# Attention followed by an MLP on one core: q and k in longer rows, group sums on VectorE, and an earlier reciprocal chain

## The chip, the cores and the metric

The kernel runs on one core of a Trainium2 chip. The metric is the device time of one execution in microseconds (us), lower is better. Timed runs of the kernel before and of another kernel alternate on the same chip. A ratio is the mean time of one kernel's fast runs over that of the other's fast runs of the same rounds, so it is not quite the ratio of the medians that stand beside it. Engine names: TensorE (PE in the profile; PEld is its weight load), VectorE (DVE), ScalarE (ACT), GpSimd (POOL), SyncE (SP).

## The reference

```python
# q, k, v: (8, 8, 576, 64) f32.  w_in: (512, 2048), w_out: (2048, 512)
q_d = q.reshape(B, H, 144, 4, D).mean(axis=3)        # the same for k_d, v_d
out_up = np.repeat(sm_attn(q_d, k_d, v_d), 4, axis=2)  # attention of group means
scores = np.where(abs(pos_i - pos_j) < 4, scale * q @ k.T, -1e9)
out_local = softmax(scores) @ v                        # a narrow band around the diagonal
x = (out_up + out_local).transpose(0, 2, 1, 3).reshape(4608, 512)
h = x @ w_in
out = (h * sigmoid(h)) @ w_out
```

## The kernel before

Heads are treated two at a time, as 32 pairs; four pairs make one batch of 576 tokens. The MLP goes over nine blocks of 512 tokens. Block 0 needs the pairs 0 to 3, block 1 the pairs 4 to 7 as well. For each pair, q and k are loaded, converted to bf16 and transposed by TensorE. First scores (the band) and second scores (of the group means), exponentials on ScalarE, a mask multiply on VectorE, row sums Z, a chain of small DMAs that turns row sums into a broadcast reciprocal, PV (probabilities by v), and the normalised xo and xT follow. In the profiles, duo is the PSUM tile of a pair's transposes, scores and PV; hps and ops are the PSUM tiles of the MLP's two matmuls; th is what ScalarE makes of hps, and gT the product that VectorE makes of both.

An engine carries out its instructions in the order in which they were written: in the traces of the kernel before, VectorE's 373 instructions come in the order of the program, by line and output tile, and so do ScalarE's 359 and, by line, SyncE's 331 DMA issues. This order is made when the kernel is built, by a small list scheduler in the kernel's own source, from a guessed duration (`cost`) of each instruction. So a wait in one engine's queue also delays whatever stands behind it.

The loads of q and k in 512-byte rows, where row c, p, r holds token 192 c + 2 p + r (two tokens of 64 values side by side):

```python
def load_qk(p):
    for nm, t, src in (("qs", qs, q), ("ks", ks, k)):
        P.op("SP", lambda s, t=t, src=src: s.dma_start(
            t[i][:, :, :], src[b, h:h + 2].rearrange("h (c p r) d -> p (h c) (r d)", p=96, r=2)), ...)
```

The transposes, the group sums by a matmul with a constant G, and the copies out of PSUM:

```python
def ph_T(p):
    for x, (nm, st, xt, xd) in enumerate((("q", qb, qT, qd), ("k", kb, kT, kd))):
        tps = D[:, x, 0:288].bitcast(BF16)
        dps = D[:, x, 288:432]
        ...   # six transposes into tps; six matmuls with G_bf into dps
        src = tps[:, :].rearrange("p (c r g) -> p c r g", c=3, r=2)
        dst = xt[j][:, :].rearrange("p (c g r) -> p c r g", c=3, r=2)   # writes every 2nd bf16: a 4-byte step
        if nm == "q":
            # VectorE: tensor_copy(dst, src), then tensor_copy(qd, dps)
        else:
            # ScalarE: activation(dst, src, Copy), then activation(kd, dps, Copy)
```

The reciprocal chain of two pairs (z): row sums to SBUF (zc), four small DMAs (zr), a reciprocal (rr), a DMA to memory (scr) and four broadcasting DMAs (Rb). All of them are issued by SyncE, which also issues all loads of q, k and v and all stores of the output:

```python
P.op("SP", ... zr[i][10*o:10*o+10, :] <- zc ...)        # four
P.op("DVE", lambda e: e.reciprocal(rr[i][:, :], zr[i][:, :]), ...)
P.op("SP", ... scr[i] <- rr[i] ...)
P.op("SP", ... Rb[n][64*h:64*h+64, :] <- scr[i][...].to_broadcast([64, 720]) ...)   # four
```

The softmax here doesn't subtract the row's maximum and nothing guards it: scores larger than these inputs give would overflow.

Of the kernel before, what the change touches and what calls it, by code (L numbers as in the profile page):

```python
# [38 lines left out]
class Prog:  # L39
# [9 lines left out]
    def __init__(self):  # L49
        self.streams = {e: [] for e in self.ENGS}  # L50
        self.know = {e: {} for e in self.ENGS}
        self.dcount = {}
        self.free = {e: 0 for e in self.ENGS}
        self.ring = {"SP": 0, "POOL": 0}
# [28 lines left out]
    def op(self, eng, fn, r=(), w=(), dma=None, cost=0):  # L83
# [24 lines left out]
        if dma:  # L108
            other = self.ring["POOL" if eng == "SP" else "SP"]
            self.free[eng] = max(t + 600, self.ring[eng] - 4000)  # L110
            begin = max(self.free[eng], self.ring[eng])
            self.ring[eng] = begin + cost + min(cost, max(0, other - begin)) // 2
# [65 lines left out]
def bass_hourglass_attn__then__act_silu_kernel(  # L178
# [9 lines left out]
    with kctx:  # L188
# [21 lines left out]
        NST, NVB, NP_, NR, NEARLY = 2, 5, 5, 4, 4  # L210
        qs = sb("qs", [96, 6, 128], F32, NST)
        ks = sb("ks", [96, 6, 128], F32, NST)
        vs = sb("vs", [128, 10, 64], F32, NST)
        vq = sb("vq", [72, 4, 256], F32, NST)
# [6 lines left out]
        kT = sb("kT", [128, S_], BF16, 2)  # L221
        qd = sb("qd", [128, SD], BF16, 2)
# [11 lines left out]
        G_bf = sb("G_bf", [96, 48], BF16)  # L234
# [26 lines left out]
        def const_g():  # L261
            pool(lambda g: g.memset(cf[0:96, 0:48], 0.25), w=[c0])
            pool(lambda g: g.affine_select(out=cf[0:96, 0:48], in_=cf[0:96, 0:48], compare_op=ALU.is_ge,
                                           fill=0.0, base=0, pattern=[[-2, 48]], channel_multiplier=1),
                 r=[c0], w=[c0])
            pool(lambda g: g.affine_select(out=cf[0:96, 0:48], in_=cf[0:96, 0:48], compare_op=ALU.is_ge,
                                           fill=0.0, base=1, pattern=[[2, 48]], channel_multiplier=-1),
                 r=[c0], w=[c0])
            pool(lambda g: g.tensor_copy(G_bf[:, :], cf[0:96, 0:48]), r=[c0], w=[R("G")])
# [17 lines left out]
        def load_qk(p):  # L287
            b, h = divmod(2 * p, H_)
            i = p % NST
            for nm, t, src in (("qs", qs, q), ("ks", ks, k)):  # L290
                P.op("SP", lambda s, t=t, src=src: s.dma_start(  # L291
                    t[i][:, :, :], src[b, h:h + 2].rearrange("h (c p r) d -> p (h c) (r d)", p=96, r=2)),
                    w=[R(f"{nm}{i}")], dma=f"{nm}{i}", cost=1100)

        def load_v(p):
            b, h = divmod(2 * p, H_)
            i = p % NST
            for hh in range(2):
# [4 lines left out]
                     w=[R(f"vs{i}")], dma=f"vs{i}", cost=900)  # L303
            P.op("SP", lambda s: s.dma_start(
                vq[i][:, :, :], v[b, h:h + 2].rearrange("h (s p r) d -> p (h s) (r d)", s=2, r=4)),
                w=[R(f"vq{i}")], dma=f"vq{i}", cost=900)

        def cast(p):
            i, j = p % NST, p % 2
            for nm, a, bb in (("q", qs, qb), ("k", ks, kb)):  # L310
                dst = bb[j][:, :, :, :]
                src = a[i][:, :, :].rearrange("p (h c) x -> p h (c x)", h=2).rearrange(
                    "p h (c d) -> p c h d", d=64)
# [10 lines left out]
        def castv(p):  # L324
            i, m = p % NST, p % NVB
# [24 lines left out]
        def ph_T(p):  # L350
            D, bk = next_duo()
            j = p % 2
            for x, (nm, st, xt, xd) in enumerate((("q", qb, qT, qd), ("k", kb, kT, kd))):
                tps = D[:, x, 0:288].bitcast(BF16)
                dps = D[:, x, 288:432]
                for c in range(3):
                    for r in range(2):
                        w = st[j][:, 2 * c + r, :, :].rearrange("p h d -> p (h d)")
                        P.op("PE", lambda t, c=c, r=r, w=w, tps=tps: t.transpose(  # L359
                            tps[:, 192 * c + 96 * r:192 * c + 96 * r + 96], w, id_bf[:, :]),  # L360
                            r=[R("id"), R(f"{nm}b{j}")], w=[bk[x]], cost=42)
                for c in range(3):
                    for r in range(2):
                        w = st[j][:, 2 * c + r, :, :].rearrange("p h d -> p (h d)")
                        mm(dps[:, 48 * c:48 * c + 48], w, G_bf[:, :], [R("G"), R(f"{nm}b{j}")],
# [414 lines left out]
```

## Time and profile before

The kernel before takes 421.43 us (median of 3 runs, 420.27 to 421.85); its profiled execution has a span of 423.5 us.

| engine | busy, us | share of the span |
|---|---|---|
| TensorE | 355.2 | 84% |
| VectorE | 243.5 | 58% |
| ScalarE | 205.2 | 48% |
| GpSimd | 155.2 | 37% |

From the page of the kernel before; the columns are line, engine, operation, output and input with their shapes, count, then busy us and the mean ns of one, then idle time of the engine before it and what ended it:

```profile
L375 ACT ACTIVATE kT<-duo 128x576 bf16<-128x576 bf16 x32 | 26.3, 821 | 39.8 <-PE duo L347 39.7
L370 DVE COPY qT<-duo 128x576 bf16<-128x576 bf16 x32 | 25.5, 796 | 12.0 <-PE duo L347 11.8
```

These are the two copies out of PSUM: 0.82 us on ScalarE and 0.80 us on VectorE, once per pair.

### The profile page before, as it was taken

What the parts mean: (1) busy time and instruction counts of PE and PEld (TensorE: products, weight loads), DVE (VectorE), ACT (ScalarE), POOL (GpSimd) and SP (SyncE); (2) the same over time, 40 slices, a digit from 0 to 9 for tenths busy, and PEclk for the clock granted to TensorE, in tenths of its full rate; (3) what the DMA queues carried; (4) which work ended last, traced back from release to release, by engine and by line L of the source; (5) the groups of instructions that cost most, each with busy time, mean ns of one, the idle gap of its engine ahead of it and who ended that gap; (6) DMA issues with size and microseconds to landing.
All of it is one profiled execution on the core that took longest, in us unless ns stands there. A gap on an engine that the chain in (4) does not pass through costs nothing.

```text
span 423.5 us, 7628 instructions
## 1 busy us (share of the span) xinstructions
PE 355.2 (84%) x3033; PEld 225.3 (53%) x3072; DVE 243.5 (58%) x373; ACT 205.2 (48%) x360; POOL 155.2 (37%) x185
## 2 busy tenths in 40 slices
PE   2441333798898979999899999999999999999996
PEld 2331222565655646666566656656556565555552
DVE  1434608777667875858776787659448334333320
ACT  4540310485645755555674756736732434434331
POOL 7634546626567452716543567117000000000000
PEclk9999999999699995999999999999999999999999
DMA  9999999698989994798985898642041100101011
GB/s 186 220 338 266 226 204 193 151 225 193 222 207 225 239 213 121 170 244 216 200 193 177 189 249 200 176 131 79 29 161 56 50 26 25 50 26 50 25 51 74
DMA packets 105665, 66.43 MB, mean 157 GB/s; under 512 B 47006, under 2 KB 95134, under 8 KB 105630
## 3 DMA queue, kind: packets, MB, share of 16 engines
q1 hardware_dynamic: 101406, 59.66, 60.4%
q0 software_dynamic: 4224, 6.29, 6.3%
q8 instruction: 24, 0.39, 0.4%
q14 instruction: 11, 0.09, 0.1%
HBM read 58.25 MB, written 9.61 MB: 160 GB/s over the span
## 4 chain that ended last, share of the span: by engine, by line
PE 64%; DMA 14%; DVE 9%; SPq 4%; issue 4%; POOL 2%; ACT 2%; POOLq 0%; ACTq 0%
PE hps L347 27%; PE ops L347 26%; PE duo L347 8%; DMA vq<-in_v_dram 7%; DMA Rb<-scr 5%; PE duo L359 3%; DVE xT L517 3%; DVE Pt L412 2%; DVE xo L498 2%; SPq L291 2%; DMA scr<-rr 1%; DVE xo L500 1%; SPq L302 1%; POOL vt L328 1%; DVE gT L542 1%
## 5 line engine op out<-in xcount | busy, mean ns | idle before, releaser
L347 PE MATMUL hps<-xT,w_in_sb 128*128 128x512 f32 x576 | 182.3, 442 | 1.7 <-DVE gT L542 1.5
L542 DVE SCALAR_TENSOR_TENSOR gT<-th,hps 128x512 bf16<-128x512 f32 x144 | 98.0, 685 | 114.6 <-ACT th L540 114.4
L347 PE MATMUL ops<-w_out_bf,gT 128*128 128x512 bf16 x537 | 139.0, 382 | 4.4 <-issue 3.3
L540 ACT ACTIVATE th<-hps 128x512 f32<-128x512 f32 x144 | 86.2, 598 | 115.3 <-PE hps L347 115.1
L347 PEld LDWEIGHTS hps<-xT,w_in_sb 128*128 128x128 f32 x576 | 108.5, 193 | 35.1 <-DVE gT L542 4.1
L347 PEld LDWEIGHTS ops<-w_out_bf,gT 128*128 128x128 bf16 x576 | 46.5, 98 | 65.6 <-issue 22.6
L326 POOL CAST vb<-vs 128x640 bf16<-128x640 f32 x32 | 24.5, 767 | 66.6 <-PE duo L347 58.6
L375 ACT ACTIVATE kT<-duo 128x576 bf16<-128x576 bf16 x32 | 26.3, 821 | 39.8 <-PE duo L347 39.7
L328 POOL TENSOR_TENSOR vt<-vq 72x512 f32<-72x512 f32 x32 | 43.2, 1349 | 6.2 <-DMA vq<-in_v_dram 6.2
L321 POOL CAST qb<-qs 96x768 bf16<-96x768 f32 x28 | 23.7, 847 | 52.6 <-PE duo L347 34.4
L517 DVE TENSOR_TENSOR xT<-xo 128x576 fp32r<-128x576 f32 (+2 forms) x40 | 39.2, 996 | 1.1
L359 PE MATMUL duo<-id_bf,qb 96*128 96x96 bf16 x192 | 16.7, 235 | 26.4 <-POOL qb L321 18.3
L412 DVE TENSOR_TENSOR Pt<-Pt,mask_bf 128x1152 bf16<-128x1152 bf16 x32 | 32.1, 1006 | 6.9 <-ACT Pt L404 6.9
L389 ACT ACTIVATE Pt<-duo 128x912 bf16<-128x912 f32 x32 | 29.8, 930 | 9.2 <-PE duo L347 9.2
L347 PE MATMUL duo<-qT,kT 64*128 64x112 bf16 (+1 forms) x320 | 21.6, 234 | 14.6 <-DVE xo L498 8.6
L330 POOL TENSOR_TENSOR vd<-vt 72x256 bf16<-72x256 f32 x32 | 31.2, 974 | 4.3
L561 ACT ACTIVATE osb<-ops 128x512 f32<-128x512 f32 x36 | 21.6, 600 | 23.0 <-PE ops L347 22.7
L370 DVE COPY qT<-duo 128x576 bf16<-128x576 bf16 x32 | 25.5, 796 | 12.0 <-PE duo L347 11.8
L359 PEld LDWEIGHTS duo<-id_bf,qb 96*128 96x128 bf16 x192 | 11.7, 113 | 34.4 <-POOL qb L321 18.9
L498 DVE TENSOR_TENSOR xo<-duo,Rb 128x456 f32<-128x456 f32 x32 | 19.9, 623 | 15.6 <-DMA Rb<-scr 10.9
L347 PEld LDWEIGHTS duo<-qT,kT 64*128 64x128 bf16 x320 | 12.2, 102 | 27.2 <-DVE xo L498 11.7
L321 POOL CAST kb<-ks 96x768 bf16<-96x768 f32 x28 | 23.6, 842 | 7.0 <-DMA ks<-in_k_dram 7.0
(55 smaller groups left out, 261.7 us busy)
## 6 DMA issues: line engine op xcount, KB each, us to landing
Rb<-scr SPq DMA_DIRECT2D x60, 180.0 KB, 4.0
vs<-in_v_dram SPq DMA_DIRECT2D x64, 160.0 KB, 5.4
qs<-in_q_dram SPq DMA_DIRECT2D x32, 288.0 KB, 5.4
ks<-in_k_dram SPq DMA_DIRECT2D x32, 288.0 KB, 6.3
vq<-in_v_dram SPq DMA_DIRECT2D x32, 288.0 KB
out_dram<-osb SPq DMA_DIRECT2D x36, 256.0 KB, 2.2
w_in_sb<-in_moe_w_in_dram POOLq DMA_DIRECT2D x4, 1024.0 KB, 13.4
w_out_bf<-in_moe_w_out_dram POOLq DMA_DIRECT2D x4, 512.0 KB, 8.8
```

Source lines behind the costliest of these rows:

```text
L321: pool(lambda g, d=dst, s=src: g.tensor_copy(d, s), r=[R(f"{nm}s{i}")], w=[R(f"{nm}b{j}")], cost=830)
L328: pool(lambda g: g.tensor_tensor(vt[:, :, :], vq[i][:, :, 0:128], vq[i][:, :, 128:256], ALU.add), r=[R(f"vq{i}")], w=[R("vt")], cost=1290)
L330: pool(lambda g: g.tensor_tensor(vd[m][:, :, :], vt[:, :, 0:64], vt[:, :, 64:128], ALU.add), r=[R("vt")], w=[R(f"vd{m}")], cost=750)
L347: return P.op("PE", lambda t: t.matmul(out_, lhsT, rhs, start=start, stop=stop, skip_group_check=True), r, w, cost=cost)
L359: P.op("PE", lambda t, c=c, r=r, w=w, tps=tps: t.transpose(tps[:, 192 * c + 96 * r:192 * c + 96 * r + 96], w, id_bf[:, :]), r=[R("id"), R( ...
L375: P.op("ACT", lambda e, src=src, dst=dst: e.activation(dst, src, AF.Copy), r=[bk[x]], w=[R(f"kT{j}")], cost=650)
L389: P.op("ACT", lambda e: e.activation(Pt[m][:, :, 0:456], D[:, :, 0:456], AF.Exp, scale=0.125), r=bk, w=[R(f"P{m}")], cost=930)
L412: P.op("DVE", lambda e: e.tensor_tensor(Pt[m][:, :, :], Pt[m][:, :, :], mask_bf[:, :].unsqueeze(1).to_broadcast([128, 2, S_]), ALU.mult), ...
L498: P.op("DVE", lambda e: e.tensor_tensor(xo[x][:, 0:456], D[:, 0, 0:456], Rb[u][:, 0:456], ALU.mult), r=[bk[0], R(f"Rb{u}")], w=[R(f"xo{x}" ...
L517: P.op("DVE", lambda e, dst=dst, in0=in0, in1=in1: e.tensor_tensor(dst, in0, in1, ALU.add), r=[R(f"xo{x}")], w=xblk(kc, t, e_), cost=180 + n)
L540: P.op("ACT", lambda e: e.activation(th[tb][:, :], hps[hb][:, :], AF.Tanh, scale=0.5), r=[R(f"h{hb}", True)], w=[R(f"th{tb}")], cost=600)
L542: P.op("DVE", lambda e: e.scalar_tensor_tensor(gT[j % 2][:, f, :], th[tb][:, :], 1.0, hps[hb][:, :], ALU.add, ALU.mult), r=[R(f"h{hb}", Tr ...
```

## The change

Its intent: fewer, longer DMA rows for q and k (1536 bytes), so that a load of q or k needs a third of the packets; q and k of the first four pairs ahead of any v; fewer matmuls, with sums of four neighbours made by VectorE from the transposed rows; and the early reciprocal chains issued from ScalarE's queue, so that they do not stand behind SyncE's loads.

With the long rows, partition p holds six neighbouring tokens (6 p to 6 p + 5), not two. The six transposes put token 6 g + r at column 96 r + g. The copy has to restore the order of the tokens, so it now writes every sixth bf16, a 12-byte step. The scale of the second exponential becomes 0.125 / 16, since sums stand in place of means on both sides.

```diff
@@ load_qk
-   t[i][:, :, :], src[b, h:h + 2].rearrange("h (c p r) d -> p (h c) (r d)", p=96, r=2)),
+   t[i][:, :, :], src[b, h:h + 2].rearrange("h (p r) d -> p h (r d)", p=96)),
@@ ph_T
-   for c in range(3):
-       for r in range(2):
-           mm(dps[:, 48 * c:48 * c + 48], w, G_bf[:, :], ..., start=(r == 0), stop=(r == 1), cost=26)
-   src = tps[:, :].rearrange("p (c r g) -> p c r g", c=3, r=2)
-   dst = xt[j][:, :].rearrange("p (c g r) -> p c r g", c=3, r=2)
-   ... DVE: qT copy, qd copy; ACT: kT copy, kd copy
+   src = [D[:, x, 0:288].bitcast(BF16).rearrange("p (r g) -> p r g", r=6) for x in range(2)]
+   dst = [t[j][:, :].rearrange("p (g r) -> p r g", r=6) for t in (qT, kT)]
+   P.op("DVE", lambda e: e.tensor_copy(dst[0], src[0]), ..., cost=800)
+   P.op("ACT", lambda e: e.activation(dst[1], src[1], AF.Copy), ..., cost=700)
+ def do_mean(p, nm):        # for q and for k
+   s4 = src[j][:, :].rearrange("p (g r) -> p g r", r=2)
+   h4 = hs[i][:, :].rearrange("p (g r) -> p g r", r=2)
+   DVE: hs <- s4[:, :, 0] + s4[:, :, 1]  (cost 370);  qd or kd <- h4[:, :, 0] + h4[:, :, 1]  (cost 220)
@@ the reciprocal chain: zr, scr and Rb
-   P.op("SP", ...
+   P.op(chain(z), ...                   # "ACT" if z < 4 else "SP"
@@ order of the loads (tasks of the scheduler)
-   wsteps = {3: (0, 1), 4: (2, 3), 5: (4,), 6: (5, 6), 7: (7,)}
-   before = {4: 'w1', 5: 'w3', 6: 'w4', 7: 'w6'}
+   wsteps = {3: (0, 1), 4: (2,), 5: (3,), 6: (4, 5), 7: (6, 7)}
+   before = {4: "lv3", 5: "w2", 6: "w3", 7: "w5", 8: "w7"}
-   lv{p} after lqk{p};  c{p} by "POOL"
+   lv{p} after lqk{max(p, 3)};  c{p} by "POOL" if p >= NEARLY else "DVE"
-   S2{p} after S1{p}
+   S2{p} after S1{p}, mq{p}, mk{p}
```

(Lines with DVE or ACT and a colon are shortened. Not shown: the scheduler's model of DMA times changed too, with other durations for the loads, a third queue, and a full in place of a half surcharge where two queues overlap. This changes only the order that it makes.)

## The prediction

> **What bounds the kernel now.** I read the summary page first (busy shares and the 40 slices), then the windows of the span, then the chain of waits in order of time, then SyncE's queue over the stretch that the chain named.
>
> The page's busy row and two of its slice rows (tenths busy, each slice 10.6 us):
>
> ```profile
> PE 355.2 (84%) x3033; PEld 225.3 (53%) x3072; DVE 243.5 (58%) x373; ACT 205.2 (48%) x360; POOL 155.2 (37%) x185
> PE   2441333798898979999899999999999999999996
> DMA  9999999698989994798985898642041100101011
> ```
>
> TensorE is full from slice 8 on; before that it idles, and there the transfers are full. The windows (busy us per engine; then granted clock, DMA share, GB/s) put numbers on it:
>
> ```profile
> 0.00:79.00 79.00, 26.02 (x371) 20.05 (x371) 37.20 (x47) 23.49 (x40) 44.93 (x68) 1.00 1.10 228
> 79.00:125.00 46.00, 43.28 (x442) 29.15 (x446) 30.45 (x49) 27.83 (x52) 23.87 (x25) 0.93 0.96 204
> 125.00:285.00 160.00, 152.73 (x1499) 98.31 (x1515) 115.19 (x186) 96.50 (x173) 78.06 (x86) 0.97 0.82 197
> 285.00:424.00 139.00, 133.16 (x732) 77.77 (x744) 60.70 (x94) 57.34 (x97) 8.31 (x8) 1.00 0.16 54
> ```
>
> The first 79 us hold 26 us of TensorE work: the MLP's first matmul (hps) starts at 78.9. Its second block of 512 tokens starts at 125.1, after PV of pair 7 at 121.7; from there TensorE is 95% busy to the end. So the end is set by when the MLP gets going plus TensorE's work after that. What holds the start, in the chain of waits (start, us, what):
>
> ```profile
> 19.27 13.85 DMA vq<-in_v_dram
> 34.45 9.08 DMA vq<-in_v_dram
> ...
> 55.36 0.54 SPq L454
> 55.94 8.82 DMA Rb<-scr
> ...
> 69.66 5.07 DVE Pt L412
> ```
>
> It is v's transfers, then the broadcast of the first reciprocals, then a mask multiply. SyncE's own queue shows why that broadcast is late:
>
> ```profile
> 20.80 3.12 SPq L437 DMA_DIRECT2D zr<-zc  x4
> ...
> 25.62 8.79 SPq L302 DMA_DIRECT2D vs<-in_v_dram  x2
> ...
> 40.05 0.44 SPq L445 DMA_DIRECT2D scr<-rr  x1
> ...
> 46.21 5.16 SPq L302 DMA_DIRECT2D vs<-in_v_dram  x2
> 51.41 3.90 SPq L304 DMA_DIRECT2D vq<-in_v_dram  x1
> 55.36 2.45 SPq L454 DMA_DIRECT2D Rb<-scr  x4
> ```
>
> Row sums out of PSUM (zc) at 18.7, reciprocal (rr) 33.2, store to scr 40.1, broadcast Rb issued 55.4, first use 64.8: 46 us, most of it behind q, k, v loads in one in-order queue. Pairs 6 and 7 again: Z at 96.2, PV at 119.9, 24 us.
>
> [...] from 22 to 36 us GpSimd's weight packets land between SP's, at 324 to 358 GB/s together against some 220 for SP alone. [...] on SP's queue 256-byte packets take 23 ns on average, 512-byte 38, 1024-byte 67. [...] the mask multiply is 0.75 us median, 1.01 mean, 5.14 longest (at 69.6, beside a run of GpSimd casts); xT of 576 averages 1.17.
>
> **The change part by part.**
>
> *q/k rows.* 1152 packets of 512 bytes per pair become 384 of 1536. All of q and k cost 36,864 x 38.07 ns / 16 engines = 87.7 us of engine time. A 1536-byte packet should lie between 67 (1024) and 90 ns (2048): my estimate 85, so 12,288 x 85 / 16 = 65 us. Saved 22 us, 0.7 per pair. Packets overlap (the share reads 1.10), so some 0.6 us of wall time per pair, and only where transfers bind: the first 8 pairs, 5 us.
>
> *Order.* q/k of pairs 0 to 3 go before any v, so transposes, scores and exponentials of four pairs no longer wait for v loads; the 8 weight loads are spread over pairs 3 to 7.
>
> *Reciprocal chain of z 0 to 3.* z 1 goes directly, so three chains of 9 DMAs move to ACT. ACT pays their issue: 4 x 0.72 (zr) + 0.38 (scr) + 4 x 0.60 (Rb) = 5.7 us each, 17 us, plus waits for landings, beside 23.5 us busy in the first 79: affordable. The 46 us from zc to first use should fall to about 15 (issue 2.9, land 3, reciprocal 0.6, scr 3, Rb issue and land 5).
>
> *Group sums.* TensorE loses 24 matmuls of 48 columns per pair; start to start they are 25 ns warm, two runs of six 0.35 us with their edges. VectorE gets four strided adds per pair[...]. ACT loses kd, 0.274 x 32 = 8.8 us. The second scores now wait for the adds, but the first scores and their exponential (0.93 us) lie between.
>
> *The sum.* When can block 1 of the MLP start (before: 125.1)? It needs PV 7, hence q, k, v of 8 pairs, all weights (pair 7's loads wait for their turn) and three broadcasts. From 2 to 20 us SP alone brought 3.3 pairs, 5.45 us each; less 0.6 makes 4.85, x 8 = 39 us. Weights: 22 to 36 us and the later stretches, less the pairs carried beside them, about 19. Broadcasts: 768 packets x 180 ns / 16, overlapped, 7. With 2 us of start and 4 of bubbles while q/k wait for two staging buffers: v 7 lands at 71. Then casts and sums of v (0.77 + 1.35 + 0.97), PV and xT: 78 at the earliest. VectorE needs by then about 8 x 4.9 (qT, adds, mask, xo, xT) + 3 (casts) + 10 (direct reciprocals) + 2 + 11 (gT of block 0) = 65 of 76 us, in a fixed order, so I add 17 for slippage: 95, 30 earlier.
>
> After that: 423.5 - 125.1 = 298.4 before. By 125 it had transposed 14 pairs, at 95 I expect 10: four pairs of transposes, scores and sums still to do, 4 x 1.4 = +6. Matmuls gone from 18 to 22 pairs x 0.35 = -7, half of which I give to a busier VectorE (72% in the third window[...]): -3. Stalls from that load: +3. So 95 + 304 = 399 in the profile; timed runs are 2 us below it (421.4 against 423.5): 397.
>
> **The rivals.** *VectorE becomes the bound*: for it, 86 to 91% and contention with GpSimd; against it, the attention runs a block ahead (PV 16 at 206.9 starts when block 2's first half ends, PV 19 at 229.4, needed at 245.6), so delays are absorbed. If true, blocks 1 to 5 keep 41 us or grow by 2: 405 to 412. *The transfers stay the bound at the start*: the DMA row is full to slice 27, so a shorter chain may only uncover the loads; for it, the weights and v are as many bytes as before. Then block 1 starts near 105 to 110: 408 to 413. *ACT's queue blocks*: its waits for landings stand in order before kT and the exponentials; each late landing (scr took 5.1 us at 142) stops attention. Three such chains at 5 us: at most +15, 410. *Everything fits*: block 1 at 80 and no stalls: 380.
>
> **Range and chances.** The gain is carried by the start (30 us, uncertain by 15) with a few us either way behind it. Two rivals together still leave some 1 to 3%. Range 381 to 414; faster by over 2% means below 413.0: 0.84; within 2%: 0.13; slower: 0.03, as that needs a stall that no part of the sum has.
>
> **What would show it.** First hps matmul at 42 to 60 instead of 78.9; second block at 85 to 105 instead of 125.1; zc to first xo about 15 us; no wait of xo for Rb of 8 us; q/k packets near 85 ns and GB/s above 220 in the first slices; VectorE busy 280 to 295; ACT near 196; TensorE 9 to 12 us less of busy G_bf matmuls' start-to-start time; the third window's block length 38 to 41 us. I am wrong if block 1 still starts after 112, or if the blocks from 1 to 5 lengthen by over 3 us each.

The sum came to 95 + 304 = 399 us in the profile, 397 timed. Cut from it is the term for the four adds per pair; its 4.9 us per pair, its 86 to 91% and its 280 to 295 us of VectorE contain that term too, and the −3 after block 1's start leans on it. An estimate from the trace of the kernel before replaces it: xT of 192 and of 576 elements took 0.346 and 0.757 us at the shortest, and a line through both gives 0.449 us for 288 elements and 0.295 for 144. Four adds are then 1.49 us per pair, 1.20 without the removed qd copy (0.284), 39 us in all; that leaves 4.9 and 280 to 295 as they are, and with 18 pairs makes 86% of the third window.

Measured, on what its text leans on: in the trace of the kernel before, two groups of VectorE's instructions took longer beside GpSimd's. The mask multiply averages 0.74 us where no GpSimd instruction runs during it (17) and 1.31 where one does (15), xT of 576 elements 0.76 (5) and 1.28 (19). The matmuls by G start every 25 ns (median) after 79 us and every 40 before. Packets of 2048 bytes took 90 ns on average on SyncE's queue, the broadcast's of 2880 bytes 162, and 206 in the first 120 us, where the prediction put 180. Its 3 us for a landing are an estimate: the chain of waits of the kernel before has one of zr of 3.15 us (at 241.8) and one of scr of 5.14. That a DMA on ScalarE's queue need not wait for SyncE's loads was an assumption then; in the changed kernel's trace, 302 packets of ScalarE's queue start between 42.4 and 52.2 us, among 1807 of SyncE's.

## More of the kernel before

In the trace of the kernel before, VectorE is idle for 5.86 us until zr has landed and rr runs at 33.20; the reciprocals Rb<-ops that stand behind it start at 33.71, though the matmuls that they read had run by 24.8.

The chain that ended last is, by engine and then by line:

```profile
PE 64%; DMA 14%; DVE 9%; SPq 4%; issue 4%; POOL 2%; ACT 2%; POOLq 0%; ACTq 0%
```

It is a chain of matmuls, with DMAs at its start and only 9% of VectorE.

## The result, and the profile after

The changed kernel takes 445.52 us (median of 4 runs, 443.05 to 449.89; the one of 449.89 is slow), beside 420.85 us for the kernel before in the same rounds. The ratio is 1.0574, with a 95% interval from 1.0504 to 1.0644: it is slower by 5.7%, where a gain of 5.8% was predicted. Executions over 1.5% slower than the fastest of the same kernel are left out of the means. The result is correct. The profiled execution has a span of 441.0 us.

The busy row of the changed kernel's page, and its row of TensorE slices, to lay beside those in the prediction:

```profile
PE 357.3 (81%) x2688; PEld 211.4 (48%) x2688; DVE 329.6 (75%) x469; ACT 236.9 (54%) x328; POOL 157.7 (36%) x181
PE   3332278686859868889789989999999999999997
```

TensorE is no busier in sum, though its program has 384 matmuls fewer (2688 weight loads, where it had 3072; 39 matmul records of the kernel before are missing). That is 12 per pair, not the 24 that the prediction writes. VectorE grew by 86 us and ScalarE by 32, where the prediction had +37 to +52 (280 to 295 in all) and −9. And the slices 8 to 27, which were full before, now read 6 to 9. The windows of the changed kernel (busy us of PE, PEld, DVE, ACT, POOL; granted clock, DMA share, GB/s):

```profile
0.00:79.00 79.00, 34.25 (x328) 22.64 (x329) 62.39 (x77) 37.63 (x44) 45.31 (x67) 0.98 1.07 237
79.00:125.00 46.00, 34.04 (x273) 18.47 (x273) 32.75 (x45) 23.09 (x31) 15.46 (x16) 0.85 0.71 173
125.00:285.00 160.00, 137.83 (x1211) 83.37 (x1208) 150.90 (x216) 106.09 (x143) 81.88 (x85) 0.96 0.73 182
```

In the first window TensorE gained 8.2 us of work. In the second it lost 9.2, in the third 14.9, and there VectorE is busy 150.9 of 160 us, that is 94%. The groups of the changed kernel's page that answer to the two copies shown of before:

```profile
L354 ACT ACTIVATE kT<-duo 128x576 bf16<-128x576 bf16 x32 | 67.8, 2120 | 23.8 <-DVE qT L353 12.4
L353 DVE COPY qT<-duo 128x576 bf16<-128x576 bf16 x32 | 66.6, 2082 | 2.9 <-PE duo L348 2.9
```

The same 128x576 elements, of the same types, on the same engines: 2.12 and 2.08 us in place of 0.82 and 0.80. That is 1.3 us more on each engine per pair, 41 us of each over 32 pairs. The chain that ended last shows that this is not beside the path:

```profile
PE 46%; DVE 34%; ACT 10%; DMA 5%; issue 3%; ACTq 1%; POOL 1%; POOLq 0%
```

VectorE and ScalarE hold 44% of it, after 11% before. By line, the copy qT alone holds 8.3% of the span, 37 us, and kT 4.7%, 21 us. The new sums were cheap where nothing disturbs them: 0.45 us (hs) and 0.31 (qd, kd) in the median, near the 0.449 and 0.295 of the estimate from xT beside the prediction. Their means are higher:

```profile
L362 DVE TENSOR_TENSOR hs<-qT 128x288 f32<-128x288 bf16 x32 | 18.0, 562 | 0.3
L364 DVE TENSOR_TENSOR qd<-hs 128x144 bf16<-128x144 f32 x32 | 16.7, 522 | 1.1
```

The two for k have 661 and 502 ns, so the four cost 2.25 us per pair where their medians make 1.52. They are longer beside GpSimd's work: where no GpSimd instruction runs during them, hs averages 0.45 us (35) and qd and kd 0.31 (39), otherwise 0.80 (29) and 0.83 (25). The first reciprocal chain, in the chain of waits of the changed kernel (start, us, what):

```profile
27.44 1.35 ACTq L427
30.32 5.13 DMA zr<-zc
36.11 5.75 DMA scr<-rr
42.44 9.77 DMA Rb<-scr
```

It runs on ScalarE's queue as meant, and takes 25.6 us from zc (26.6) to the first xo (52.2), down from 46, but its DMAs land in 5 to 10 us, not in the 3 to 5 that the prediction allowed.

TensorE starts block 0 of the MLP at 60.9 us (before: 78.9) and block 1 at 131.5 (before: 125.1). What is left after the start of block 1 takes 309.5 us (before: 298.4).

### The profile page after: what moved, and what is told of

It reads as the page before. It is cut to its first block, busy times and chain, and to the rows that moved or that the text cites. A ratio compares the mean times of both kernels' runs of the same rounds, so it can differ in the third digit from the quotient of the medians.

```text
span 441.0 us, 6955 instructions
## 1 busy us (share of the span) xinstructions
PE 357.3 (81%) x2688; PEld 211.4 (48%) x2688; DVE 329.6 (75%) x469; ACT 236.9 (54%) x328; POOL 157.7 (36%) x181
## 3 DMA queue, kind: packets, MB, share of 16 engines
q1 hardware_dynamic: 75480, 57.38, 52.2%
## 4 chain that ended last, share of the span: by engine, by line
PE 46%; DVE 34%; ACT 10%; DMA 5%; issue 3%; ACTq 1%; POOL 1%; POOLq 0%
PE hps L338 21%; PE ops L338 19%; DVE qT L353 8%; DVE gT L532 6%; DVE hs L362 5%; ACT kT L354 5%; PE duo L338 4%; DVE Pt L399 3%; ACT th L530 3%; DVE xT L507 3%; DVE xo L488 3%; DVE qd L364 2%; DMA Rb<-scr 2%; PE duo L348 2%; DVE kd L364 1%
## 5 line engine op out<-in xcount | busy, mean ns | idle before, releaser
L338 PE MATMUL hps<-xT,w_in_sb 128*128 128x512 f32 x576 | 180.7, 441 | 10.9 <-DVE gT L532 10.5
L338 PE MATMUL ops<-w_out_bf,gT 128*128 128x512 bf16 x576 | 149.3, 389 | 0.0
L530 ACT ACTIVATE th<-hps 128x512 f32<-128x512 f32 x144 | 88.9, 623 | 103.2 <-PE hps L338 96.8
L354 ACT ACTIVATE kT<-duo 128x576 bf16<-128x576 bf16 x32 | 67.8, 2120 | 23.8 <-DVE qT L353 12.4
L353 DVE COPY qT<-duo 128x576 bf16<-128x576 bf16 x32 | 66.6, 2082 | 2.9 <-PE duo L348 2.9
L317 POOL CAST vb<-vs 128x640 bf16<-128x640 f32 x32 | 27.0, 845 | 70.7 <-PE duo L338 46.5
L507 DVE TENSOR_TENSOR xT<-xo 128x576 fp32r<-128x576 f32 (+2 forms) x40 | 31.7, 808 | 1.1
L321 POOL TENSOR_TENSOR vd<-vt 72x256 bf16<-72x256 f32 x32 | 29.4, 918 | 4.1
L338 PEld LDWEIGHTS duo<-qT,kT 64*128 64x128 bf16 x320 | 11.7, 101 | 39.0 <-issue 13.2
L399 DVE TENSOR_TENSOR Pt<-Pt,mask_bf 128x1152 bf16<-128x1152 bf16 x32 | 28.9, 904 | 1.5 <-ACT Pt L391 1.5
L391 ACT ACTIVATE Pt<-duo 128x240 bf16<-128x240 f32 x32 | 12.4, 388 | 29.5 <-PE duo L338 23.8
```

The costliest lines, as they stand in the source:

```text
L321: pool(lambda g: g.tensor_tensor(vd[m][:, :, :], vt[:, :, 0:64], vt[:, :, 64:128], ALU.add), r=[R("vt")], w=[R(f"vd{m}")], cost=750)
L338: return P.op("PE", lambda t: t.matmul(out_, lhsT, rhs, start=start, stop=stop, skip_group_check=True), r, w, cost=cost)
L353: P.op("DVE", lambda e: e.tensor_copy(dst[0], src[0]), r=[bk[0]], w=[R(f"qT{j}")], cost=800)
L354: P.op("ACT", lambda e: e.activation(dst[1], src[1], AF.Copy), r=[bk[1]], w=[R(f"kT{j}")], cost=700)
L399: P.op("DVE", lambda e: e.tensor_tensor(Pt[m][:, :, :], Pt[m][:, :, :], mask_bf[:, :].unsqueeze(1).to_broadcast([128, 2, S_]), ALU.mult), ...
L507: P.op("DVE", lambda e, dst=dst, in0=in0, in1=in1: e.tensor_tensor(dst, in0, in1, ALU.add), r=[R(f"xo{x}")], w=xblk(kc, t, e_), cost=180 + n)
```

## The experiments

There were 18 runs. "The comparison" is the check of the output against the reference. It is blunt here: the scores of these inputs are near zero and the softmax nearly uniform, so it called two kernels correct that hold q and k in the wrong order (e1, e4). The labels with "wrong" mark kernels meant as measurements only.

The table holds what the text uses of each. "Idle" is the length of a stretch less TensorE's busy time in it, from the windows of each profiled execution; "rest" is the span less the start of block 1. In most of these traces 36 to 40 of the 576 records of the second MLP matmul are missing, about half of them between 125 and 285 us (in those of the changed kernel, e19 and e20 none are), so idle times of a trace can be too high by a few us; the rows that the argument compares most closely (before, e2, e6, e7, e8, e13) all lack 36 to 40.

| kernel | median us | ratio to before, 95% interval | blocks 0 / 1 start | rest | TensorE busy | idle 0–79 | idle 79–125 | idle 125–285 | idle total |
|---|---|---|---|---|---|---|---|---|---|
| before | 420.9 | 1 | 78.9 / 125.1 | 298.4 | 355.2 | 53.0 | 2.7 | 7.3 | 68.3 |
| after | 445.5 | 1.057 (1.050, 1.064) | 60.9 / 131.5 | 309.5 | 357.3 | 44.8 | 12.0 | 22.2 | 83.7 |
| e1_contig_wrong | 419.7 | 0.993 (0.985, 1.002) | 56.9 / 119.7 | 293.3 | 345.9 | 40.8 | 11.7 | 10.1 | 67.1 |
| e2_read_strided | 420.7 | 0.997 (0.989, 1.005) | 55.6 / 124.3 | 296.2 | 350.9 | 41.1 | 13.2 | 10.7 | 69.6 |
| e4_before_step12_wrong | 436.3 | 1.032 (1.022, 1.041) | 79.7 / 130.2 | 304.2 | 352.4 | 53.6 | 7.0 | 15.7 | 82.0 |
| e5_rows512 | 422.8 | 1.004 (0.995, 1.012) | 57.1 / 123.5 | 296.1 | 347.8 | 41.4 | 14.2 | 11.7 | 71.8 |
| e6_before_chain | 426.5 | 1.008 (1.004, 1.013) | 81.3 / 118.0 | 307.9 | 354.8 | 49.8 | 8.3 | 7.9 | 71.1 |
| e7_before_order | 424.8 | 1.006 (1.000, 1.012) | 65.9 / 122.0 | 300.3 | 357.2 | 43.3 | 5.8 | 10.9 | 65.1 |
| e8_before_chain_order | 426.5 | 1.008 (1.001, 1.014) | 58.6 / 123.6 | 303.0 | 357.4 | 41.4 | 9.1 | 14.0 | 69.2 |
| e9_true_costs | 459.2 | 1.087 (1.080, 1.094) | 70.8 / 137.9 | 317.8 | 358.2 | 49.4 | 8.8 | 27.5 | 97.4 |
| e10_no_chain_wrong | 426.6 | 1.006 (1.000, 1.012) | 52.2 / 121.5 | 304.0 | 351.1 | 37.1 | 15.1 | 17.3 | 74.4 |
| e11_quarter_weights_wrong | 416.6 | 0.985 (0.980, 0.990) | 53.9 / 119.0 | 295.1 | 348.6 | 39.2 | 11.4 | 10.3 | 65.5 |
| e12_both_wrong | 418.4 | 0.987 (0.982, 0.993) | 51.0 / 112.0 | 303.9 | 349.3 | 35.6 | 10.0 | 16.0 | 66.6 |
| e13_lat5 | 426.2 | 1.007 (1.001, 1.013) | 54.4 / 117.2 | 303.4 | 349.8 | 39.4 | 9.0 | 16.5 | 70.8 |
| e15_sums_rows | 430.2 | 1.017 (1.013, 1.021) | 71.0 / 124.9 | 303.6 | 349.3 | 49.0 | 7.9 | 17.2 | 79.2 |
| e16_order_only | 426.3 | 1.010 (1.005, 1.015) | 61.7 / 123.7 | 297.6 | 350.0 | 44.8 | 9.8 | 11.8 | 71.3 |
| e17_store_pool | 432.0 | 1.020 (1.015, 1.026) | 57.7 / 125.4 | 306.4 | 351.6 | 42.3 | 13.9 | 16.0 | 80.2 |
| e18_sums_rows512 | 435.2 | 1.028 (1.023, 1.033) | 70.9 / 126.1 | 303.6 | 350.7 | 48.2 | 8.8 | 16.9 | 79.0 |
| e19_deep | 430.9 | 1.021 (1.016, 1.027) | 55.1 / 124.0 | 305.7 | 358.1 | 39.5 | 13.0 | 15.5 | 71.6 |
| e20_before_deep | 425.2 | 1.007 (1.002, 1.011) | 76.5 / 115.5 | 307.3 | 358.0 | 49.3 | 4.6 | 7.2 | 64.8 |

### The two copies

The theory was that the 12-byte write step of the two copies makes the loss. Its rivals were that VectorE's sums, the chain on ScalarE or the new order make it, and that the scheduler, which still counts 800 and 700 ns for the copies, merely puts work in a bad order.

**e1_contig_wrong.** The changed kernel, whose copies write without a step and leave the tokens in the wrong order.

```diff
-   src = [... .rearrange("p (r g) -> p r g", r=6) ...];  dst = [... .rearrange("p (g r) -> p r g", r=6) ...]
+   src = [D[:, x, 0:288].bitcast(BF16) for x in range(2)]
+   dst = [t[j][:, :] for t in (qT, kT)]
```

> The changed kernel with the two copies out of PSUM (qT on VectorE, kT on ACT) writing their 576 columns side by side instead of 12 bytes apart; the values are then in the wrong order, so the result is wrong on purpose; every instruction, its place and its waits stay. Theory 1 (the 12-byte write step makes each copy 1.3 us longer, and that load on VectorE and ACT is the loss): qT falls from 2.08 to about 0.8 us and kT from 2.12 to about 0.8, VectorE's busy time from 330 to about 285, and the time comes to 395 to 420. Theory 2 (the four added sums per pair overload VectorE): copies fall but the time stays at 430 or more. Theory 3 (the new order of loads or ACT's queue blocks): time stays at 435 or more, with the copies short.

Measured: 419.72 us (415.01 to 420.97), ratio 0.9933. The copies take 0.44 us on VectorE and 0.65 us on ScalarE:

```profile
L354 ACT ACTIVATE kT<-duo 128x576 bf16<-128x576 bf16 x32 | 20.7, 648 | 24.6 <-issue 13.5 <-PE duo L348 11.1
L353 DVE COPY qT<-duo 128x576 bf16<-128x576 bf16 x32 | 14.1, 440 | 1.8 <-PE duo L348 1.8
```

The programs of TensorE, GpSimd and SyncE are the same as in the changed kernel, and in the traces VectorE and ScalarE, too, carry out the same instructions in the same order. So nothing but the copies differs: they carry the whole loss.

**e2_read_strided.** The same, but with a correct result: the copies read PSUM in steps of 96 elements (192 bytes), six at a time, and write SBUF without a step.

```diff
-   rearrange("p (r g) -> p r g", r=6)      # source;  destination "p (g r) -> p r g"
+   rearrange("p (r g) -> p g r", r=6)      # source;  destination "p (g r) -> p g r", in order
```

> The changed kernel with the same two copies walking the destination in order and the PSUM source in steps of 96 columns (192 bytes), so that the result stays right. Theory 1, if only the write side minds its step: copies 0.75 to 0.9 us, time within 1% of the run with contiguous copies. If a stepped read of PSUM costs as much as a stepped write of SBUF: copies 1.5 to 2.2 us and time 430 to 450. Theories 2 and 3: no change, 440 to 446.

Measured: 420.72 us (418.06 to 422.57), ratio 0.9972, correct. The groups of e2's page:

```profile
L354 ACT ACTIVATE kT<-duo 128x576 bf16<-128x576 bf16 x32 | 20.7, 648 | 24.8 <-DVE qT L353 13.2
L353 DVE COPY qT<-duo 128x576 bf16<-128x576 bf16 x32 | 23.7, 740 | 2.6 <-PE duo L348 2.6
```

The step costs nothing on ScalarE when it is on the reading side (648 ns, as in e1), and 0.30 us on VectorE. The 25 us between the changed kernel and this one come from which side of the copy has the step. VectorE is now busy 293.2 us and ScalarE 195.4, which is what the prediction had (280 to 295 and 196).

**e4_before_step12_wrong.** The kernel before, with nothing altered but the write step of its copies, from 4 to 12 bytes (tokens in the wrong order).

```diff
-   src = tps[:, :].rearrange("p (c r g) -> p c r g", c=3, r=2);  dst = xt[j] ... "p (c g r) -> p c r g", c=3, r=2
+   src = tps[:, :].rearrange("p (r g) -> p r g", r=6);           dst = xt[j] ... "p (g r) -> p r g", r=6
```

> The kernel before with nothing changed but the write step of its two copies: 12 bytes instead of 4 (wrong result on purpose). Theory 1: qT and kT go from 0.80 and 0.82 to about 2.1 us, VectorE's busy time from 244 to about 285, and the time rises by 5 to 25 us (425 to 446), less than in the changed kernel since VectorE has no sums to do. Theories 2 and 3: the copies may lengthen, but the time stays within 1% of 421.

Measured: 436.3 us (432.43 to 441.14), ratio 1.0316. From its page:

```profile
L375 ACT ACTIVATE kT<-duo 128x576 bf16<-128x576 bf16 x32 | 67.8, 2119 | 31.2 <-PE duo L347 31.0
L370 DVE COPY qT<-duo 128x576 bf16<-128x576 bf16 x32 | 66.7, 2084 | 8.2 <-PE duo L347 8.2
```

The durations are those of the changed kernel to 2 ns, without long rows, sums, chain or order. In the timed medians, the step costs the kernel before 15 us (436.3 − 421.25, same rounds) and the changed one 25 us (445.5 − 420.7, of different rounds). A likely reason for the difference, not tested by itself, is that VectorE has the sums besides in the changed kernel.

**e9_true_costs.** The changed kernel, with the scheduler told the true durations.

```diff
-   w=[R(f"qT{j}")], cost=800)      w=[R(f"kT{j}")], cost=700)
+   w=[R(f"qT{j}")], cost=2080)     w=[R(f"kT{j}")], cost=2120)
```

> The changed kernel as it is, 12-byte write steps included, but with its scheduler told the two copies' measured durations (2080 and 2120 ns instead of 800 and 700), so only the order of instructions differs. If the loss is a schedule made for wrong durations: 420 to 432. If it is the load itself on VectorE and ACT: 436 to 450, within 2% of the changed kernel.

Measured: 459.16 us, ratio 1.0869, slower still. A better estimate in the scheduler does not bring the time back; the order that it makes costs another 3%. In e1 and e2, which keep the order built on the wrong numbers, the time does come back. So the loss is the load on the engines, and the rival falls.

### The parts one by one

With fast copies the changed kernel only equals the one before. The prediction had 24 us of gain, so half of the question was still open. These runs take the parts singly.

**e5_rows512.** The changed kernel with the old 512-byte rows, so that the 4-byte write step comes back.

```diff
-   qs, ks: [96, 2, 384];  "h (p r) d -> p h (r d)", p=96;  copies with r=6
+   qs, ks: [96, 6, 128];  "h (c p r) d -> p (h c) (r d)", p=96, r=2;  copies with c=3, r=2
```

> The changed kernel with only its rows undone: q and k again as 512-byte rows, so the copies write 4 bytes apart; sums on VectorE, order of loads, ACT's queue and the order of all instructions stay. Theory 1: copies about 0.8 us, time 398 to 428; slower than the run with contiguous copies and 1536-byte rows by what the longer packets were worth, 2 to 10 us. Theory 2 or 3: 430 or more.

Measured: 422.79 us, ratio 1.0038 (e2 of the same rounds: 0.9972). The long rows are worth 0.7% here, with intervals that overlap. The pair e15 and e18 below, which also have one order of instructions, gives 1.1%, with intervals that don't touch. Both differences hold the copies' own times besides (kT 0.65 us with long rows and stepped reads, 0.82 with short rows).

**e6_before_chain, e7_before_order, e8_before_chain_order.** The kernel before with the chain on ScalarE's queue, with the new load order, and with both.

```diff
 e6, e8:
-   P.op("SP", ... zr), P.op("SP", ... scr), P.op("SP", ... Rb)
+   P.op("ACT" if z < 4 else "SP", ...)
 e7, e8:
-   the old wsteps, before, lv and c tasks
+   the new ones
```

> The kernel before with one part of the change alone: the DMAs of the first three reciprocal chains issued from ACT's queue instead of SyncE's (the instruction order is made anew by the kernel's own scheduler). If SyncE's in-order queue was what held the first broadcast: first use of Rb at 30 to 45 us instead of 64.8, first MLP matmul at 50 to 65 instead of 78.9, the second block earlier than 125 by 5 to 20, time 402 to 418. If the chain only waits elsewhere: second block within 4 us of 125, time within 1% of before.

> The kernel before with the new order of loads alone (q and k of pairs 0 to 3 ahead of v, weights spread over pairs 3 to 7; rows of 512 bytes, sums by matmuls, reciprocal chain on SyncE). My theory: the chain still queues behind loads, so the first MLP matmul stays at 65 to 85 and the time at 412 to 424. Rival: the order itself is the cost or the gain, over 2% either way.

> Both of these on the kernel before: the change without its longer rows and without the sums on VectorE. Against the run of the change with 512-byte rows (422.8) it differs by the sums alone. If the sums on VectorE hold up pairs 4 to 7 (there PE waited for kd, and VectorE stood behind a reciprocal that waited for its DMA): second block at 95 to 115 instead of 123.5, time 395 to 412. If the start is bound by transfers or by the reciprocal chain itself: second block 118 to 126, time 415 to 424, and the sums then cost nothing net.

Measured: 426.48 us (ratio 1.0083), 424.75 (1.0058) and 426.45 (1.0077). None is a gain; the intervals of e6 and e8 lie above 1. In e6 the first broadcast reciprocal is used at 42.5 us, 22 earlier than before (64.8), but block 0 does not start earlier: PV of pair 3 comes at 78.2, although its q and k had landed by 22.9, its v was being converted from 29.9, and the last of its own reciprocals ends at 71.2. In TensorE's fixed order it stands behind the transposes of pair 8 (76.6). These wait for a cast by GpSimd, which stands behind work on v that lands at 73.7. In e7 and e8 block 0 does start 13 and 20 us earlier. The table shows where that goes: against the kernel before, e8 has 11.6 us less idle TensorE before 79 us, and 6.4 and 6.7 more in the two stretches after. The totals are 68.3 (before), 71.1, 65.1 and 69.2. The idle time is moved, hardly removed, and this with VectorE no busier than before (67% of the stretch from 79 to 285, where it was 71%). So the lost gain isn't VectorE's load alone.

**e15_sums_rows, e16_order_only, e18_sums_rows512.** From e2 and e5, parts taken away: e15 is the kernel before with long rows (stepped reads) and sums on VectorE, without order and chain; e18 the same with 512-byte rows, thus the sums alone, but for the scheduler's new model of DMA times, which e15 to e18 keep and e6 to e8 don't have; e16 is e2 with the chain back on SyncE.

```diff
 e15, e16, e18:
-   return "ACT" if z < 4 else "SP"
+   return "SP"
 e15, e18 also:
-   the new wsteps, before, lv and c tasks
+   the old ones
```

> The kernel before with only two parts of the change: long rows of q/k with the copies reading PSUM in steps and writing contiguously, and the group sums on VectorE. The old load order and SyncE's chain of reciprocals stay. If the order and the ACT chain are what costs TensorE its time between block 0 and block 1 (they each made the kernel before 0.6 and 0.8% slower), this beats both: block 1 at 118 to 123, rest after it 293 to 297, 413 to 417 us, ratio 0.980 to 0.990. If the stall there is only the load on VectorE (sums), this is no better than 420.7: ratio 0.997 or more.

> The changed kernel with stepped reads (e2_read_strided), but every reciprocal chain back on SyncE's queue: the new load order stays. e6_before_chain and e2_read_strided differ in what surrounds the chain; if the chain on ACT costs time of itself there (ACT waits in order for landings), this is 1 to 3 us faster than 420.7 and block 0 still starts at 60 to 68: ratio 0.990 to 0.995. If the ACT chain is what brings the early start its worth, this is slower: ratio 1.000 to 1.010.

> As e15_sums_rows, but with the old 512-byte rows and the 4-byte write step: the group sums on VectorE alone, on top of the kernel before. From e5 against e8 the sums are worth 7 us after block 1, of which the busier VectorE may take part before it: 415 to 419, ratio 0.985 to 0.995. The difference to e15_sums_rows is what the rows are worth in the old order: 2 to 4 us.

Measured: 430.16 us (ratio 1.0170), 426.26 (1.0097) and 435.16 (1.0282). The first theory of e15 fell: leaving out order and chain makes it worse, not better, and there is no version here that beats both kernels. In e16 block 0 starts 6 us later than in e2, and the time is 1.3% more (of different rounds, and the intervals just touch), so a gain from the chain on ScalarE is likely there but not clear of noise. The sums alone (e18), for which a gain of 0.5 to 1.5% was expected, cost 2.8%, although they take matmuls off TensorE (busy 350.7 us, where it was 355.2): its idle time is 4.8 us less before 79 us and 15.5 more after it. With the new order and the chain, the same sums cost nothing that can be seen (e5 1.0038, e8 1.0077, of different rounds and with different models of DMA times). So the parts do not add up: the order and the chain are a small loss without the sums (e8 against before) and a gain of some 2% with them (e5 against e18).

### What holds block 1

In e2 block 0 starts 23 us earlier than before, and block 1 at 124.3, as before (125.1). The windows of e2:

```profile
0.00:79.00 79.00, 37.85 (x361) 25.73 (x364) 57.03 (x79) 29.34 (x47) 47.67 (x68) 0.98 1.08 245
79.00:125.00 46.00, 32.82 (x280) 18.70 (x284) 32.95 (x51) 17.66 (x32) 19.86 (x21) 0.86 0.68 173
125.00:285.00 160.00, 149.26 (x1303) 93.38 (x1322) 139.21 (x238) 92.25 (x157) 82.30 (x88) 0.97 0.79 192
```

From 79 to 125 us TensorE, VectorE and the DMA engines (share 0.68, where it was 0.96) all have idle time, so none of these is full there; that they wait for each other is the reading that the next lines support. The timeline of VectorE in e2 shows one such wait (start, us, engine, line, operation, tiles; in brackets the idle time before it and what ended it):

```profile
87.41 0.69 DVE L532 SCALAR_TENSOR_TENSOR gT<-th,hps 128x512 bf16<-128x512 f32 x1 [1.54 <-ACT th L530]
89.65 0.59 DVE L433 RECIPROCAL rr<-zr 40x72 f32<-40x72 f32 x1 [1.56 <-DMA zr<-zc]
91.24 1.28 DVE L532 SCALAR_TENSOR_TENSOR gT<-th,hps 128x512 bf16<-128x512 f32 x2 [0.99 <-ACT th L530]
92.44 0.45 DVE L362 TENSOR_TENSOR hs<-qT 128x288 f32<-128x288 bf16 x1
...
93.64 0.31 DVE L364 TENSOR_TENSOR kd<-hs 128x144 bf16<-128x144 f32 x1
```

The sums of pair 7 (92.4 to 93.9) stand in VectorE's queue behind the reciprocal rr, which waits for zr to land at 89.6, and behind gT of block 0. The transposes of pair 7 had run at 69.1 to 69.8 and its first scores at 73.5 to 81.0. Second scores of pair 7 follow at 94.0, row sums of pairs 6 and 7 at 101.4, the copy zc at 102.4, first xo of that chain at 118.2, block 1 at 124.3.

**e10_no_chain_wrong, e11_quarter_weights_wrong, e12_both_wrong.** From e2: reciprocals of the early chains read from v without waiting for the row sums' chain; only a quarter of the weights loaded (and used again); both.

```diff
 e10, e12:
-   Rb <- scr[i][...].to_broadcast([64, 720]), after r{z}
+   Rb <- v[a, h] broadcast, after Z{z}, for z < 4
 e11, e12:
-   w_in_sb[:, :, 512 * c:512 * c + 512] <- moe_w_in[:, ...];  w_out_bf[:, 4 * c:4 * c + 4, :] <- ...
+   w_in_sb[:, 0:1, 512 * c:512 * c + 512] <- moe_w_in[0:128, ...];  w_out_bf[:, 4 * c:4 * c + 1, :] <- ...
```

> The change with the stepped-read copies (420.7), and for the first reciprocal chains the broadcast Rb read from rows of v, without waiting for the reciprocals (wrong result on purpose; the chain itself still runs, nobody waits for it). The second block of the MLP starts at 124 there although the first starts at 56. If two reciprocal chains one after the other (pairs 4 and 5, then 6 and 7, some 20 us each) hold the second block: it starts at 95 to 110, time 392 to 408. If transfers or the fixed order hold it: 115 to 124, time 412 to 421.

> The change with the stepped-read copies, loading only a quarter of each weight piece and using that quarter four times (wrong result on purpose; same matmuls, same order of instructions). This takes some 14 us of transfers out of the first 80. If transfers hold the second block: it starts at 105 to 115 instead of 124, time 402 to 412. If the reciprocal chains hold it: 119 to 125, time 415 to 421.

> Both at once. If either alone is the bound, this equals the better of the two within 3 us; if both bind in turn, it is better than each: second block at 85 to 100, time 383 to 400.

Measured: 426.63 us (ratio 1.0059), 416.57 (0.9849) and 418.35 (0.9874), with wrong results. In e10 block 1 starts at 121.5. But e10 does not take the chain out of the way: its reciprocal rr still stands in VectorE's queue before the sums of pair 7, and VectorE still waits there for zr. From its timeline:

```profile
92.25 0.59 DVE L433 RECIPROCAL rr<-zr 40x72 f32<-40x72 f32 x1 [3.77 <-DMA zr<-zc]
92.77 0.46 DVE L362 TENSOR_TENSOR hs<-qT 128x288 f32<-128x288 bf16 x1
```

So it only shows what the broadcast's wait for the reciprocals is worth, in an order made anew; whether the chain holds block 1 is left open. With a quarter of the weights it starts at 119.0, although v of pair 7 is converted 11 us earlier (55.5, in e2 66.5). Only both together bring it to 112.0, and then the rest lengthens from 296.2 to 303.9 us. e11 has the order of instructions of e2, and there the earlier block 1 does shorten the whole, by 1% (416.6, where e2 has 420.7, of different rounds); in e10 and e12 the scheduler made a new order.

**e13_lat5.** From e2: the scheduler counts 5.0 us from the end of a DMA's transfer to its landing.

```diff
-   op.end = self.ring[eng] + 1800
+   op.end = self.ring[eng] + 5000
```

> The change with the stepped-read copies, right result, with the scheduler told that a DMA lands 5.0 us after its data instead of 1.8 (measured landings of the chain's small DMAs in the first 120 us: 5 to 7.6 us). Only the order of instructions changes. If the fixed order built on too early landings makes the in-order queues wait: second block at 105 to 118, time 403 to 415. If not: within 1% of 420.7.

Measured: 426.24 us, ratio 1.0065. The timeline of VectorE in e13 fits the reading above of the late sums (the whole order was made anew, so it is no test of that wait alone):

```profile
80.78 0.45 DVE L362 TENSOR_TENSOR hs<-qT 128x288 f32<-128x288 bf16 x1
...
81.98 0.31 DVE L364 TENSOR_TENSOR kd<-hs 128x144 bf16<-128x144 f32 x1
...
84.07 0.58 DVE L433 RECIPROCAL rr<-zr 40x72 f32<-40x72 f32 x1
```

The sums of pair 7 now stand before the reciprocal. Second scores of pair 7 come at 82.3 (e2: 94.0), row sums at 85.9 (101.4), block 1 at 117.2 (124.3). But the rest takes 303.4 us (296.2), and the span is the same (420.6 and 420.5).

**e17_store_pool.** From e2: the output stores issued by GpSimd, so that SyncE's loads do not stand behind the first output rows.

```diff
-   P.op("SP", lambda s: s.dma_start(out[row:row + 128, :], osb[s_][:, :]),
+   P.op("POOL", lambda s: s.dma_start(out[row:row + 128, :], osb[s_][:, :]),
```

> e2_read_strided with the output stores issued by GpSimd instead of SyncE, so that q/k/v loads of pairs 9 to 12 do not stand behind the first output rows at 85 to 98 us. If that wait of SyncE's queue is what holds block 1, the DMA share between 79 and 125 rises from 0.68 to 0.85 or more and block 1 starts at 114 to 119: ratio 0.983 to 0.992. If VectorE's order or the reciprocal chains hold it, block 1 stays at 122 to 126 and the time within 2 us of 420.7; it can get slower, as GpSimd's casts then stand behind the output waits.

Measured: 431.99 us, ratio 1.0204. The DMA share from 79 to 125 us is 0.69, as in e2, and block 1 starts at 125.4. The stores in SyncE's queue are not what holds it.

**e19_deep, e20_before_deep.** From e2 and from the kernel before: six buffers for the exponentials (Pt, Pd) in place of five.

```diff
-   NVB, NP_, NR = 5, 5, 4
+   NVB, NP_, NR = 5, 6, 4
```

> e2_read_strided with six buffers in place of five for the exponentials (Pt, Pd), so that the first scores of pair p wait for PV of pair p-6. In e2 TensorE is idle 13 of the 46 us from 79 to 125, and the first scores of pair 9 start only at 105.9, after PV of pair 4 at 97.7, the buffer that they wait for. If that depth holds it, the first scores of pair 9 start before 90, TensorE's busy time in this window rises from 32.8 to 37 or more, and the time falls to 412 to 417, ratio 0.978 to 0.988, a version that beats both kernels. If VectorE (in order, 86% busy from there) holds it, the work goes elsewhere and the time stays within 3 us of 420.7: ratio 0.990 to 1.004.

> The control: the kernel before with the same six buffers. TensorE has only 2.7 us idle in that window there, so nothing is to be gained in it: 419 to 424, ratio 0.993 to 1.005 by both theories. If this gains as much as e19_deep does over e2_read_strided, the depth has nothing to do with the stall that the change made.

Measured: 430.85 us (ratio 1.0212) and 425.2 (1.0065). In e19 the first scores of pair 9 start at 104.5 (e2: 105.9), so they did not wait for that buffer (in e2, too, they come 8 us after PV of pair 4); the transposes of pair 9 start at 92.9, just behind the second scores of pair 7 (92.6), which the sums hold up. e20 is the more telling of the two: on the kernel before, one more buffer moves block 1 from 125.1 to 115.5, 9.6 us earlier, and the time does not fall at all, since the rest grows from 298.4 to 307.3.

## Why the prediction was wrong

**The step that made the loss.** "VectorE gets four strided adds per pair" and "ACT loses kd": the sum counts what is added to and taken from the two engines, and takes their remaining instructions as unchanged. The copies qT and kT keep their shape, type and engine, but the long rows force another order of their writes. That term was left out: 1.29 us per pair on VectorE and 1.30 on ScalarE. It is shown by e1 and e2 (taken away: −25 us of the timed medians) and by e4 (given to the kernel before: +15 us over its 421). This is the step by which the change became slower and not merely no faster. For a write step of 2, 4 and 12 bytes, the copy of 128x576 bf16 from PSUM to SBUF took 0.44 us (e1), 0.80 (before) and 2.08 (the changed kernel, e4) on VectorE, and 0.65, 0.82 and 2.12 on ScalarE; the reading of PSUM had no step in any of these. Why a longer step takes longer is not shown; the runs show the durations alone.

**The start of block 1.** "v 7 lands at 71 ... PV and xT: 78 at the earliest ... so I add 17 for slippage: 95". Landing was estimated well: v of pair 7 is converted from 68.8 us in the changed kernel and from 66.5 in e2. The slippage was wrong. From there to block 1, e2 takes 58 us, not 24. The step took the landing of v as the last thing to wait for, and everything between as fitting in. But pairs 4 to 7 have to go through VectorE's fixed queue one after another, and the second of two reciprocal chains starts (zc 102.4) only after the first (zc 79.0, first xo 100.7). Less transfer (e11) moves block 1 by 5 us, a broadcast that doesn't wait (e10) by 3, sums ahead of the reciprocal (e13) by 7, both of the first two by 12. No single edit tried here frees it, and which wait holds it stays open.

**"95 + 304".** This sum assumes that an earlier block 1 shortens the whole. Where the order of instructions stays that of e2, it does: in e11 block 1 starts at 119.0 and the rest takes 295.1 us (e1: 119.7 and 293.3), where e2 has 124.3 and 296.2. In four kernels with an order made anew it did not: in e6, e12, e13 and e20 block 1 starts at 112 to 118, and the rest takes 303 to 308 us. But the rest is as long, 303 to 306 us, with block 1 at 123.6 to 126.1 in e8, e15, e17, e18 and e19. So it isn't shown that the early start is what lengthens it; in all of these nine the order was made anew. The prediction allowed +6 for attention still to be done and counted the rest of the 30 us as gain. The span is TensorE's busy time plus its idle time, and order and chain left the idle time where it was: 68.3 us before, 69.2 in e8, 69.6 in e2.

**Slips in its sums.** "TensorE loses 24 matmuls" should be 12 per pair, as the difference of the two programs shows (384 in all); its "two runs of six", from which the gain was worked out, are right. That "timed runs are 2 us below it" is a misreading: in every run the timed figure is about 2 us above its span (1.7 to 2.2; 425.2 against 423.5 for the profiled run of the kernel before), and that run just took longer than the median of 421.4. Both are small beside the miss.

**What was right.** The rivals: VectorE does become the bound of the third stretch with the slow copies (94%), and 87% with fast ones, within the 86 to 91% estimated; the blocks 1 to 5 lengthen by 2.4 us each in the changed kernel (41.3, where they took 38.9), and not at all in e2 (38.6). Block 0 starts at 55.6 in e2, within 42 to 60 (60.9 in the changed kernel, just outside). Packets of 1536 bytes took 95 ns on average in the first 120 us of the changed kernel and 93 later, against the estimate of 85. The chain took 24 us in e2 and 25.6 in the changed kernel, not 15: the mechanism (out of SyncE's queue) was right, the landings were underestimated. ScalarE's queue did not block in a way that e6 could show beyond 0.8%. Matmuls taken off: TensorE is busy 9.6 us less in e5 than in e8, within the 9 to 12 named.

**What stays open.** From 125 to 285 us TensorE is idle 7 to 8 us in the kernels with neither the new load order nor the sums (before, e6, e20), 11 to 14 with the order and without the sums (e7, e8), 17 with the sums and without the order (e15, e18), and 10 to 17 with both and fast copies. Which of the queue waits there binds was not settled; the order is remade whenever a duration or a dependency changes, and this can move the time by 1 to 3% (e9 against the changed kernel; e13, e17 and e19 against e2). No version with a right result beat the kernel before clearly: e2 equals it within its interval.

One rival to all of this is tested by no run: TensorE's granted clock. It averages 0.991 in the fast timed runs of the kernel before that list it (37 of them, 0.983 to 1.000), 0.967 in those of e2 and 0.963 in those of the changed kernel. In the traces TensorE is busy 15.8 us (before), 23.9 us (e2) and 25.2 us (the changed kernel) in spells granted half speed; the MLP's first matmuls start every 0.23 us outside of them and every 0.43 inside (medians, before and changed kernel alike). An estimate from this: close to half of the difference, some 4 us, is lost in e2's trace beyond what before's loses, and up to 10 us (0.024 of 420) in the timed runs. That is too little for the prediction's 24 us, and it can't explain the copies, as e2 and the changed kernel have nearly the same clock. But part of why e2 gains nothing may lie there.

## What to carry to other kernels

When a layout of loads changes, look at each instruction that restores the order further on, and at its step in bytes on the writing side, above all when its shape and place in the list of groups do not change; put the step on the reading side where a run shows that it costs less there (here 0.74 us on VectorE and 0.65 on ScalarE in e2, for 2.08 and 2.12 with the step on the writing side). When an early stage is made to start sooner, ask what work TensorE will have at the new time: an idle gap that moves from before a stage to behind it is no gain, so sum idle time over the whole span and don't take the start of one stage as a stand-in for the end. Try the parts alone before the whole, as they need not add up: here the sums without the order and the chain cost 2.8%, the order and the chain without them 0.8%, and all parts together, with fast copies, nothing.
